# Preparing the factors of a Strassen product earlier and in smaller pieces, in a kernel of attention and two feed-forward networks

## The chip, the core and the metric

The kernel runs on one core of a Trainium2 chip. The metric is the device time of one execution in microseconds (us). Median, lowest and highest of three runs are given, and one further execution was profiled.

## The reference

Attention with keys and values pooled by eight, then a product of two linear layers, then a softplus network. All in float32; eight of the inputs are drawn eight times larger.

```python
k_p = k.reshape(B, H, Sp, 8, D).mean(axis=3); v_p = v.reshape(B, H, Sp, 8, D).mean(axis=3)
attn = softmax(q @ k_p.T / sqrt(D)) @ v_p          # B=8, H=8, S=576, D=64
x = attn.transpose(0, 2, 1, 3).reshape(4608, 512)
a = x @ w1; b = x @ w2                             # d_ff = 1024
x2 = (a * b @ w3) @ w_out                          # 512 wide
h = x2 @ w_in                                      # d_ff = 2048
out = (maximum(h, 0) + log1p(exp(-abs(h)))) @ w_out2
```

## The kernel before, in words

Every large product is made of three matmuls (`mm3`, L120): each operand is split into a rounded high part (copied by ScalarE, ACT) and the remaining low part (subtracted by VectorE, DVE), the pair that `split` (L115) issues. The weights arrive as 64-bit words and are converted by a chain of ACT and DVE operations.

**Phase 1** goes through nine blocks `j` of 512 tokens, each in eight units `i`. A unit (`p1_step`, L490) is 24 matmuls of 512 columns for a and b (`ab`, L455), then 12 matmuls of `x2_mm` (L475) for the unit before; w3 and w_out are multiplied into one matrix W at the start. a is copied from PSUM by ACT (L466), multiplied with b by DVE (L469) and split again. At the end of a block four results x2 are copied out (L485, L487) and stored to DRAM (L488). Between the three parts of a unit lie three slots. A slot calls what the hand-written list `sched` holds for it (attention of a later block) and then a number of steps of `background`, a list of generators whose step ends at each `yield`: `slot_1` (L500) makes one or two steps in turn, `bg_3` (L668) two or three. The list `sched` ends with unit 5 of block 7 (`i7` = 5). From there on the background is `late_jobs` (L613): eight `wi_job` (L566), which convert w_in, form the seven left factors of Strassen's method for one of eight column groups `t`, split them and store them to DRAM (`wis`), and eight `wo2_job` (L596), which convert w_out2. A `wo2_job` waits until the units of block 8 that read its memory are done. Before phase 2, L684 makes all remaining steps up to the fourth `wo2_job`.

**Phase 2** (loop at L766) goes through 48 steps `n`: six superblocks `s` of 768 tokens, eight groups `t` each. A step has seven products of six matmuls with 384 columns (`product`, L701), which accumulate in turn in the two PSUM tiles X and Z, and parts of the last product (`o_part`, L734), six matmuls of 512 columns each. After product 0, X is copied by ACT to a snapshot (L781) before product 2 may go on in X; after product 1, Z is added by DVE (L786) before product 3 may go on in Z, and so on (L797, L804, L809, L815, L822). The softplus of the step before (`soft_ops`, L712) runs on ACT and DVE meanwhile. Left factors come from DRAM by DMAs that GpSimd issues (`load_factors`, L535).

The seven right factors of a superblock come from x2, loaded by `x2_load` (L629) at t = 1, in steps of `x2_steps` (L650): four subtractions of 768 columns and seven splits. They lie in eight places of a ring. Three of the steps come at the end of t = 3, 4 and 5, the other six all within t = 7 (`xstep`, L771). In step n = 0 the last twelve matmuls of `x2_mm` stand ahead of product 2:

```python
                if n == 0:
                    next(xs)
                    x2_mm(NB - 1, K1 - 1)
                    load_factors(1, 1)
                product(n, 2)
                nc.scalar.activation(snap[1], xz[0], AF.Copy)
```

Every engine works its instructions off in the order written; loads and stores other than those of the left factors are issued by SyncE (SP), whose queue is in order too.

Of the kernel before, what the change touches and what calls it, by code (L numbers as in the profile page):

```python
# [15 lines left out]
P = 128  # L16
# [32 lines left out]
def pooled_attention_two_ffn(ctx: ExitStack, tc: tile.TileContext, qT_d, kT_d, v_d, w12_d, w3T_d, wo_d, wi_d, wo2_d, out):  # L49
# [141 lines left out]
    def add_group(src, slot, name, into):  # L191
# [8 lines left out]
        add_job(name, [src[:, 2 * i:2 * i + 2, :] for i in range(2)], dst)  # L200

# [172 lines left out]
    with tc.manual_schedule():  # L374
# [74 lines left out]
        background += [next_job() for _ in range(5)]  # L449
# [40 lines left out]
        def p1_step(j, i, slots):  # L490
# [5 lines left out]
            if (j, i) != (0, 0):  # L496
                x2_mm(*((j, i - 1) if i else (j - 1, K1 - 1)))
# [28 lines left out]
        F8 = F2 // 2 // P  # L526


        wis = [[dram.tile([P, 2, n, 256], F32, name=f"wis{t}_{n}", tag=f"wis{t}_{n}") for n in (3, 4)] for t in range(F8)]
        fin = ctx.enter_context(tc.tile_pool(name="fin", bufs=1))  # L530
        wf = fin.tile([P, 20 * 256], F32R, tag="wf", name="wf")
        y2 = fin.tile([P, 1024], F32, tag="y2", name="y2")
        wgroup = {}

        def load_factors(n, i):  # L535
            if n < F8 * NS:
                w = mem(GBUF + 8, [P, 2048], F32R) if (n % 2, i) == (1, 1) else wf[:, (0, 1536, 3584)[2 * (n % 2) + i]:][:, :(1536, 2048)[i]]
                wgroup[n, i] = w.rearrange("p (h c f) -> p h c f", h=2, f=256)
                nc.gpsimd.dma_start(wgroup[n, i], wis[n % F8][i].bitcast(F32R))

        t2k_ring[0] = Ring([T2K + 8 + 2 * i for i in range(4)])
        wo2_hl = {}


        EARLY = F8 + 4

        def load_rawl(n, srcs):
            raw = mem(RAW if n >= EARLY or n % 2 == 0 else RAW + 8, [P, 1024, 2], I32)
            n = 1024 // len(srcs)
            for i, src in enumerate(srcs):  # L550
                nc.sync.dma_start(raw[:, n * i:n * i + n, :].rearrange("p n t -> p (n t)"), src.bitcast(I32))
            return raw

        def convert_1024(raw, y):
            yi = y.bitcast(I32)
            nc.scalar.activation(y, raw[:, :, 1].bitcast(F32), AF.Abs, scale=HI_SCALE)
            yield
            nc.vector.tensor_scalar(y, y, HI_MIN, HI_MAX, op0=ALU.max, op1=ALU.min)
            nc.vector.tensor_scalar(yi, yi, 3, None, op0=ALU.logical_shift_left)
# [331 lines left out]
```

## Time and profile before

| | |
|---|---|
| median of three runs | 1651.43 us |
| lowest and highest | 1647.8 and 1652.45 us |
| the profiled execution | 1652.47 us |
| its span, from first to last instruction | 1650.7 us |
| PE busy in the span | 1551.8 us (94%), 7712 matmuls |
| DVE, ACT busy | 1001.8 us (61%), 786.6 us (48%) |
| mean granted TensorE clock | 0.978 |

Times in views count from the span's start. PE is TensorE's matmul stream, PEld its weight loads. A busy time of PE is modelled and overlaps, so the distance between starts of matmuls is the better measure. PEclk is the clock that was granted to TensorE, as a share of full speed.

### The profile page before, as it was taken

What the parts mean: (1) busy time and instruction counts of PE and PEld (TensorE: products, weight loads), DVE (VectorE), ACT (ScalarE), POOL (GpSimd) and SP (SyncE); (2) the same over time, 40 slices, a digit from 0 to 9 for tenths busy, and PEclk for the clock granted to TensorE, in tenths of its full rate; (3) what the DMA queues carried; (4) which work ended last, traced back from release to release, by engine and by line L of the source; (5) the groups of instructions that cost most, each with busy time, mean ns of one, the idle gap of its engine ahead of it and who ended that gap; (6) DMA issues with size and microseconds to landing.
All of it is one profiled execution on the core that took longest, in us unless ns stands there. A gap on an engine that the chain in (4) does not pass through costs nothing.

```text
span 1650.7 us, 20063 instructions
## 1 busy us (share of the span) xinstructions
PE 1551.8 (94%) x7712; PEld 1297.0 (79%) x7712; DVE 1001.8 (61%) x1490; ACT 786.6 (48%) x1651; POOL 53.6 (3%) x104
## 2 busy tenths in 40 slices
PE   4899999999999999898858999999999999999998
PEld 2457888888888887776647888898988988898997
DVE  7886534243423343348777877676677777677665
ACT  3454433343334343334345565556555555556554
POOL 0000000000000000000000000000000000000000
PEclk9999999999999999999978999999999999999999
DMA  8752212021202120219846435334434533533431
GB/s 272 223 164 72 89 35 87 18 85 35 75 21 74 35 75 1 77 58 354 276 141 209 134 115 178 122 108 155 145 117 145 171 116 120 180 109 115 147 115 39
DMA packets 64416, 198.44 MB, mean 120 GB/s; under 512 B 6464, under 2 KB 21824, under 8 KB 57152
## 3 DMA queue, kind: packets, MB, share of 16 engines
q1 hardware_dynamic: 50496, 109.07, 20.1%
q0 software_dynamic: 13824, 88.09, 16.4%
q8 instruction: 61, 1.00, 0.3%
q14 instruction: 35, 0.29, 0.1%
HBM read 163.58 MB, written 33.55 MB: 119 GB/s over the span
## 4 chain that ended last, share of the span: by engine, by line
PE 63%; DVE 19%; ACT 10%; DMA 5%; issue 2%; SPq 1%; DVEq 0%; ACTq 0%
PE ab L122 7%; PE ab L124 6%; PE ab L123 6%; PE o L747 5%; PE o L746 5%; PE o L745 5%; DVE area_r L118 4%; PE x2p L122 3%; PE x2p L124 3%; PE x2p L123 3%; PE X L122 3%; PE X L124 3%; PE X L123 3%; ACT area_r L117 2%; ACT area_f L717 2%; PE pv L303 2%
## 5 line engine op out<-in xcount | busy, mean ns | idle before, releaser
L117 ACT ACTIVATE area_r<-area_f 128x768 fp32r<-128x768 f32 (+1 forms) x168 | 126.7, 754 | 244.5 <-DVE area_f L469 175.8
L747 PE MATMUL o<-w2h,area_r 128*128 128x512 f32 x576 | 229.4, 398 | 0.3 <-DVE area_r L118 0.3
L746 PE MATMUL o<-w2l,area_r 128*128 128x512 f32 x576 | 228.8, 397 | 0.0
L745 PE MATMUL o<-w2h,area_r 128*128 128x512 f32 x576 | 225.8, 392 | 0.0
L118 DVE TENSOR_TENSOR area_r<-area_f,area_r 128x768 fp32r<-128x768 f32 (+1 forms) x168 | 141.7, 844 | 110.4 <-ACT area_r L117 110.2
L717 ACT ACTIVATE area_f<-area_f 128x768 f32<-128x768 f32 x96 | 81.3, 847 | 122.3 <-DVE area_f L815 120.8
L747 PEld LDWEIGHTS o<-w2h,area_r 128*128 128x128 f32 x576 | 109.0, 189 | 24.0 <-DVE area_r L118 0.7
L122 PE MATMUL X<-area_r,wf 128*128 128x384 f32 x288 | 100.8, 350 | 26.3 <-ACT xr L781 18.0
L745 PEld LDWEIGHTS o<-w2h,area_r 128*128 128x128 f32 x576 | 109.2, 190 | 16.2 <-ACT area_r L117 0.3
L746 PEld LDWEIGHTS o<-w2l,area_r 128*128 128x128 f32 x576 | 109.0, 189 | 16.0
L122 PE MATMUL x2p<-area_r 128*128 128x512 f32 x288 | 116.6, 405 | 5.2 <-ACT area_r L117 4.0
L469 DVE TENSOR_TENSOR area_f<-area_f,ab 128x512 f32<-128x512 f32 x72 | 49.4, 686 | 106.7 <-PE ab L124 105.0
L123 PE MATMUL x2p<-area_r 128*128 128x512 f32 x288 | 113.1, 393 | 0.2 <-DVE area_r L118 0.2
L124 PE MATMUL x2p<-area_r 128*128 128x512 f32 x288 | 113.2, 393 | 0.0
L268 ACT ACTIVATE pr<-sc,mx 128x72 f32<-128x72 f32 x288 | 87.7, 331 | 47.1 <-DVE mx L266 47.0
L118 DVE TENSOR_TENSOR area_r<-pv,area_r 128x512 fp32r<-128x512 f32 x36 | 24.8, 689 | 136.4 <-ACT area_r L117 136.4
L123 PE MATMUL X<-area_r,wf 128*128 128x384 f32 x288 | 99.3, 345 | 0.0
L124 PE MATMUL X<-area_r,wf 128*128 128x384 f32 x288 | 99.2, 345 | 0.0
L726 DVE SCALAR_TENSOR_TENSOR area_f<-area_f 128x768 f32<-128x768 f32 x96 | 91.3, 951 | 0.0
L466 ACT ACTIVATE area_f<-ab 128x512 f32<-128x512 f32 x72 | 43.1, 598 | 90.3 <-PE ab L124 65.8
L122 PEld LDWEIGHTS X<-area_r,wf 128*128 128x128 f32 x288 | 55.5, 193 | 37.3 <-ACT xr L781 20.6
L718 ACT ACTIVATE area_f<-area_f 128x768 f32<-128x768 f32 x96 | 81.2, 846 | 3.1
(190 smaller groups left out, 3468.1 us busy)
## 6 DMA issues: line engine op xcount, KB each, us to landing
wf<-wis POOLq DMA_DIRECT2D x48, 768.0 KB, 4.6
wf<-wis POOLq DMA_DIRECT2D x24, 1024.0 KB, 5.2
area_r<-wis POOLq DMA_DIRECT2D x24, 1024.0 KB, 5.1
area_f<-in_wo_dram SPq DMA_DIRECT2D x24, 512.0 KB
kv<-in_kT_dram SPq DMA_DIRECT2D x32, 288.0 KB
q<-in_qT_dram SPq DMA_DIRECT2D x18, 512.0 KB
kv<-in_v_dram SPq DMA_DIRECT2D x32, 288.0 KB
x2d<-area_f SPq DMA_DIRECT2D x36, 256.0 KB
```

The lines of the kernel that those rows point to most:

```text
L117: nc.scalar.activation(hi, src, AF.Copy)
L118: nc.vector.tensor_sub(lo, src, hi.bitcast(F32))
L122: nc.tensor.matmul(ps, whi, xhi, start=first, stop=False, skip_group_check=resumed)
L123: nc.tensor.matmul(ps, whi, xlo, start=False, stop=False, skip_group_check=resumed)
L124: nc.tensor.matmul(ps, wlo, xhi, start=False, stop=last, skip_group_check=resumed)
L268: nc.scalar.activation(pr[:, h, :], sc[h // 4][:, h % 4, :], AF.Exp, bias=mx[:, h:h + 1], scale=SCALE, accum_out=sm[:, h:h + 1])
L717: nc.scalar.activation(e, c, AF.Abs)
L718: nc.scalar.activation(e, e, AF.Exp, scale=-1.0)
L726: nc.vector.scalar_tensor_tensor(c, c, 0.0, e, op0=ALU.max, op1=ALU.subtract)
L745: nc.tensor.matmul(oacc[s][i], hl[:, 0, ts], wh, start=first, stop=False)
L746: nc.tensor.matmul(oacc[s][i], hl[:, 0, ts], wl, start=False, stop=False)
L747: nc.tensor.matmul(oacc[s][i], hl[:, 1, ts], wh, start=False, stop=last)
```

## The change

The left factors are prepared by a new generator `left_factors` in the background of phase 1, behind the last conversions of w1 and w2, in halves of 512 columns with two stage buffers, and their loads and the first x2 load are issued when attention ends. From then on the ring of phase 1's temporaries has four places and not eight. `bg_3` is gone: the last eleven units use `slot_1`. The generator `wo2_jobs` converts w_out2 for t = 0 to 5 there and in a loop ahead of phase 2, and for t = 6, 7 in halves during phase 2. Of block 8's `x2_mm`, units 4 to 7 are not run in phase 1 but as eight halves in the places that `o_part` leaves empty in steps 0 and 1. The right factors are spread: one step of `x2_steps` each in t = 3, 4, 5 and 6, three in t = 7, two in t = 0 of the next superblock; the ring has a ninth place. The snapshots and x2's halves have tiles of their own.

```diff
+    wis = [[dram.tile([P, 2, n, 256], F32, name=f"wis{t}_{n}", tag=f"wis{t}_{n}") for n in (3, 4)] for t in range(F8)]
...
+    def left_factors():
+        t2k_ring[0] = Ring([T2K + 8 + 2 * i for i in range(4)])
...
+        for _ in range(8):
+            yield
+        nc.sync.dma_start(raw.rearrange("p n t -> p (n t)"), wi_d[0].rearrange("p q k f -> p (q k f)").bitcast(I32))
+        yield
+        for t in range(F8):
+            yield from convert_1024(raw, y)
+            if t + 1 < F8:
+                nc.sync.dma_start(raw.rearrange("p n t -> p (n t)"), wi_d[t + 1].rearrange("p q k f -> p (q k f)").bitcast(I32))
+            a11, a12, a22, a21 = (y[:, 256 * i:256 * i + 256] for i in range(4))
+            s2, s3, s1, s4 = (S[:, 256 * i:256 * i + 256] for i in range(4))
+            nc.vector.tensor_add(s1, a21, a22)
+            nc.vector.tensor_sub(s3, a11, a21)
+            yield
+            nc.vector.tensor_sub(s2, s1, a11)
+            nc.vector.tensor_sub(s4, a12, s2)
+            yield
+            w3_, w4_ = wis[t]
+            for src, dsts in (
+                (y[:, :512], [w3_[:, :, 0:2, :]]),
+                (y[:, 512:768], [w4_[:, :, 2, :]]),
+                (S[:, :512], [w3_[:, :, 2, :], w4_[:, :, 0, :]]),
+                (S[:, 512:], [w4_[:, :, 1, :], w4_[:, :, 3, :]]),
+            ):
+                n = src.shape[1]
+                st = stage([P, 2, 512])[:, :, :n]
+                hi = st[:, 0, :].bitcast(F32R)
+                nc.scalar.activation(hi, src, AF.Copy)
+                yield
+                nc.vector.tensor_sub(st[:, 1, :].bitcast(F32R), src, st[:, 0, :])
+                n //= len(dsts)
+                for i, dst in enumerate(dsts):
+                    dst = dst.rearrange("p h c f -> p h (c f)") if len(dst.shape) == 4 else dst
+                    nc.sync.dma_start(dst, st[:, :, n * i:n * i + n])
+                yield
...
-        background += [next_job() for _ in range(5)]
+        background += [next_job() for _ in range(5)] + [left_factors()]
...
-        def x2_mm(j, i):
+        def x2_mm(j, i, ms=range(KD)):
...
-            hi, lo = g_hl.pop((j, i))
-            for m in range(KD):
+            hi, lo = g_hl[j, i]
+            for m in ms:
...
-                    sb = t2k(f"x2s{j}_{m}")
+                    sb = o_ring([P, 512]) if j == NB - 1 else t2k(f"x2s{j}_{m}")
...
-            if (j, i) != (0, 0):
+            if (j, i) != (0, 0) and (j, i) <= (NB - 1, K1 // 2):
                 x2_mm(*((j, i - 1) if i else (j - 1, K1 - 1)))
...
-        wf = fin.tile([P, 20 * 256], F32R, tag="wf", name="wf")
-        y2 = fin.tile([P, 1024], F32, tag="y2", name="y2")
+        wf = fin.tile([P, 2, 7 * 512], F32R, tag="wf", name="wf")
...
+        c_ring = {0: Ring([0, 3]), 1: Ring([6])}
+        e_ring, us = Ring([9, 12]), (mem(15, [P, TS]), mem(18, [P, TS]))
+        o_ring = Ring([21, 23])
...
-        EARLY = F8 + 4
...
-        def wi_job(t, raw):
...
-        def wo2_job(t, raw):
-            while (NB - 1, 2 * (t // 2) + 1) not in p1_done:
...
+        def wo2_jobs(ts, ys, raws, parts):
...
+            seq = [(t, p) for t in ts for p in parts]
...
+            for n, (t, p) in enumerate(seq):
+                while (NB - 1, 2 * (t // 2) + 1) not in p1_done:
+                    yield
+                raw, y = raws[n % len(raws)], ys[n % len(ys)]
+                yield from convert_1024(raw, y)
...
+                hi, lo = (w[:, p[0]:p[-1] + 1, :].rearrange("p i f -> p (i f)") for w in w2)
+                nc.scalar.activation(hi, y, AF.Copy)
                 yield
...
+                nc.vector.tensor_sub(lo, y, hi.bitcast(F32))
...
-        xq_ring = Ring([XODD + 6 * i for i in range(8)])
+        xq_ring = Ring([XODD + 6 * i for i in range(8)] + [GBUF + 8])
...
-        def bg_3():
-            att = slot_now[0]
-            slot_now[0] += 1
-            bg((2, 3)[att % 2])
+        load_factors(0, 0)
+        load_factors(0, 1)
+        load_factors(1, 0)
+        load_factors(1, 1)
+        x2_load(0)
+        background.append(wo2_jobs(range(6), [mem(T2K, [P, 1024]), mem(T2K + 4, [P, 1024])], [mem(RAW + 8 * i, [P, 1024, 2], I32) for i in range(2)], [(0, 1)]))
         for i in range(i7, K1):
-            p1_step(NB - 2, i, [bg_3] * 3)
-        xs = None
+            p1_step(NB - 2, i, [slot_1] * 3)
+        xs = x2_steps(0)
         for i in range(K1):
-            p1_step(NB - 1, i, [bg_3] * 3)
+            p1_step(NB - 1, i, [slot_1] * 3)
             p1_done.add((NB - 1, i))
-            if i >= 4 and xr:
-                xs = xs or x2_steps(0)
-                for _ in range(3):
-                    if len(xq.get(0, [])) < 5:
-                        next(xs)
-        while late_done[0] < EARLY:
+            for _ in range((2, 1, 1, 0, 1, 1, 1, 0)[i]):
+                next(xs)
+        while background:
             bg(1)
+        background.append(wo2_jobs((6, 7), [mem(25, [P, 512])], [mem(27, [P, 512, 2], I32)], [(0,), (1,)]))
+        rest = [(i, ms) for i in range(K1 // 2, K1) for ms in ((0, 1), (2, 3))]
...
-        o_ring = Ring([RAW + 14, T2K, T2K + 2])
...
+            if n < 0 and rest:
+                i, ms = rest.pop(0)
+                x2_mm(NB - 1, i, ms)
...
-                oacc[s] = [acc_tile(f"o{s}_{i}") for i in range(4)] + [mm_tile(f"o{s}_{i}") for i in (4, 5)]
+                oacc[s] = [mm_tile(f"o{s}_{i}") for i in range(2)] + [acc_tile(f"o{s}_{i}") for i in range(2, TT)]
...
             s, t = divmod(n, F8)
             h = n < NH
-            last_t = t == F8 - 1 and s + 1 < NS
-            def xstep():
-                if last_t:
-                    next(xs)
+            if n == 2:
+                o_ring = Ring([21, 23, 25, 27, 29])
+            if h and t == 3 and s + 1 < NS:
+                xs = x2_steps(s + 1)
+            def factors(*when):
+                if h and t in when and (s if t < 3 else s + 1) < NS:
+                    next(xs, None)
...
                 product(n, 0)
                 nc.scalar.activation(snap[0], xz[0], AF.Copy)
+                factors(0)
             soft_step(n - 1, 0)
             soft_step(n - 1, 1)
             if h:
                 product(n, 1)
                 nc.vector.tensor_add(soft[n, 0][:, :HS], snap[0], xz[1])
-                xstep()
             o_part(n - 2, 0, 0)
+            factors(0, 7)
...
             o_part(n - 2, 0, 2)
+            factors(3, 4, 5, 6, 7)
...
             o_part(n - 1, 1, 1)
             soft_step(n, 1)
             soft_step(n, 0)
             o_part(n - 1, 1, 2)
+            factors(7)
             bg(1)
-            if h and s + 1 < NS:
-                if t == 1:
-                    x2_load(s + 1)
-                if t == 3:
-                    xs = x2_steps(s + 1)
-                if t in (3, 4, 5):
-                    next(xs)
+            if h and t == 1 and s + 1 < NS:
+                x2_load(s + 1)
```

## Rows read from the trace of the kernel before

**Rows 1.** Windows: us; PE, PEld, DVE, ACT, POOL busy (count); PEclk; DMA share; GB/s

```profile
125.00:200.00 75.00, 72.60 (x405) 59.47 (x404) 47.10 (x90) 36.44 (x116) 0.00 (x0) 0.98 0.24 76
200.00:650.00 450.00, 450.00 (x2448) 369.35 (x2447) 168.47 (x304) 168.00 (x579) 0.00 (x0) 1.00 0.17 52
...
722.11:837.07 114.96, 98.47 (x397) 78.68 (x396) 85.75 (x115) 41.61 (x52) 1.72 (x3) 0.93 0.75 257
837.07:889.06 51.99, 30.96 (x115) 26.16 (x114) 37.43 (x45) 26.12 (x37) 2.65 (x5) 0.77 0.54 183
889.06:988.33 99.27, 95.85 (x469) 83.78 (x467) 79.99 (x101) 58.74 (x83) 6.67 (x12) 1.00 0.40 135
```

**Rows 2.** Waits of PE, 722.11 to 889

```profile
PE ab L122 <- ACT area_f L466: 11.7, 3, 6.6
PE X L122 <- ACT xr L781: 8.7, 1, 8.7
PE X L122 <- DVE area_f L809: 5.5, 2, 5.2
```

**Rows 3.** Timeline of PE, 24 matmuls apart: start us, us, line

```profile
640.86 0.39 PE L122 MATMUL ab<-area_r,w_6h 128*128 128x512 f32 x1
...
646.30 0.39 PE L122 MATMUL x2p<-area_r 128*128 128x512 f32 x1
```

**Rows 4.** Windows of steps n=8, 9 and 24, columns as in group 1

```profile
988.33:1007.76 19.43, 17.58 (x78) 15.44 (x79) 13.15 (x18) 11.23 (x16) 1.06 (x2) 0.91 0.27 89
1007.76:1023.40 15.64, 15.64 (x79) 14.07 (x78) 11.46 (x16) 8.90 (x15) 1.05 (x2) 1.00 0.74 233
...
1246.73:1264.75 18.02, 16.16 (x79) 14.01 (x79) 12.76 (x17) 10.71 (x15) 1.38 (x2) 1.00 0.32 101
```

**Rows 5.** Groups by line, shapes apart: xcount, busy us, mean ns of one

```profile
L118 DVE TENSOR_TENSOR area_r<-area_f,area_r 128x512 fp32r<-128x512 f32 x72 | 49.8, 692 | 55.5 <-ACT area_r L117 55.5
L469 DVE TENSOR_TENSOR area_f<-area_f,ab 128x512 f32<-128x512 f32 x72 | 49.4, 686 | 106.7 <-PE ab L124 105.0 <-ACT kT L234 1.1 <-ACT area_f L466 0.5
...
L118 DVE TENSOR_TENSOR area_r<-xr,area_r 128x768 fp32r<-128x768 f32 x42 | 40.0, 954 | 31.5 <-ACT area_r L117 31.5
...
L117 ACT ACTIVATE area_r<-xr 128x768 fp32r<-128x768 f32 x42 | 34.8, 832 | 8.8 <-DMA xr<-x2d 8.8
...
L561 DVE SCALAR_TENSOR_TENSOR area_f<-area_f 128x1024 int32<-128x1024 int32 x12 | 14.7, 1222 | 0.2
...
L556 ACT ACTIVATE area_f<-area_f 128x1024 f32<-128x1024 f32 x12 | 13.6, 1135 | 1.3 <-DVE w2l L607 0.6 <-DMA area_f<-in_wi_dram 0.4 <-DMA area_f<-in_wo_dram 0.3
...
L607 DVE TENSOR_TENSOR w2l<-area_f,w2h 128x1024 fp32r<-128x1024 f32 x8 | 9.8, 1220 | 3.4 <-ACT w2h L603 3.4
...
L603 ACT ACTIVATE w2h<-area_f 128x1024 fp32r<-128x1024 f32 x8 | 8.4, 1055 | 18.6 <-DVE area_f L563 18.6
...
L558 DVE TENSOR_SCALAR area_f<-area_f 128x1024 f32<-128x1024 f32 x12 | 8.3, 689 | 6.7 <-ACT area_f L556 6.7
```

**Rows 6.** Timeline around the first wait for a snapshot

```profile
856.81 0.47 ACT L781 ACTIVATE xr<-X 128x384 f32<-128x384 f32 x1
...
857.33 0.69 PE L122 MATMUL X<-area_r,wf 128*128 128x384 f32 x1 [8.74 <-ACT xr L781]
...
861.34 0.37 PE L122 MATMUL X<-area_r,wf 128*128 128x384 f32 x1
```

**Rows 7.** Chain of waits at 861 us and at the end: start, us

```profile
861.53 6.54 DMA x2d<-area_f
...
1643.98 2.09 DMA out_dram<-area_f
```

**Rows 8.** Timeline of DVE in step n = 12

```profile
1059.47 0.55 DVE L786 TENSOR_TENSOR area_f<-xr,Z 128x384 f32<-128x384 f32 x1
```

**Rows 9.** Timeline of PE in step n = 6

```profile
962.39 0.44 PE L122 MATMUL Z<-area_r,wf 128*128 128x384 f32 x1 [1.08 <-DVE area_f L786]
```

**Rows 10.** Chain of waits at 755 us

```profile
755.91 6.21 DMA wis<-wih
```

More of the change, by code (lines that the diff above doesn't have):

```diff
@@ L536, in load_factors @@
             if n < F8 * NS:
-                w = mem(GBUF + 8, [P, 2048], F32R) if (n % 2, i) == (1, 1) else wf[:, (0, 1536, 3584)[2 * (n % 2) + i]:][:, :(1536, 2048)[i]]
-                wgroup[n, i] = w.rearrange("p (h c f) -> p h c f", h=2, f=256)
+                wgroup[n, i] = wf[:, n % 2, 1536 * i:1536 + 2048 * i].rearrange("p (h c f) -> p h c f", h=2, f=256)
                 nc.gpsimd.dma_start(wgroup[n, i], wis[n % F8][i].bitcast(F32R))
-        t2k_ring[0] = Ring([T2K + 8 + 2 * i for i in range(4)])
@@ L542, in pooled_attention_two_ffn @@
         wo2_hl = {}
-        EARLY = F8 + 4
[L547 to L559, printed above, removed]
-            yield
-            nc.vector.scalar_tensor_tensor(yi, raw[:, :, 1], -0x80000000, yi, op0=ALU.bitwise_and, op1=ALU.bitwise_or)
-            yield
-            nc.vector.scalar_tensor_tensor(yi, raw[:, :, 0], 29, yi, op0=ALU.logical_shift_right, op1=ALU.bitwise_or)
-            yield
@@ L596, in wo2_job @@
-        def wo2_job(t, raw):
-            while (NB - 1, 2 * (t // 2) + 1) not in p1_done:
-                yield
-            y = mem(T2K + 4 if t % 2 and t < EARLY - F8 else T2K, [P, 1024])
-            yield from convert_1024(raw, y)
-            hi, lo = (main.tile([P, 2, 512], F32R, tag=f"wg{x}{t}", name=f"w2{x}{t}") for x in "hl")
-            nc.scalar.activation(hi.rearrange("p i f -> p (i f)"), y, AF.Copy)
-            for i in range(2):
-                wo2_hl[t + F8 * i] = hi[:, i, :], lo[:, i, :]
-            yield
-            nc.vector.tensor_sub(lo.rearrange("p i f -> p (i f)"), y, hi.rearrange("p i f -> p (i f)").bitcast(F32))
@@ L609, in pooled_attention_two_ffn, with load_wo2 @@
-        late = [(wi_job, t, [wi_d[t].rearrange("p q k f -> p (q k f)")]) for t in range(F8)]
-        late += [(wo2_job, t, [wo2_d[(t + F8 * i) * P:(t + F8 * i + 1) * P, :] for i in range(2)]) for t in range(F8)]
-        late_raw, late_done = [], [0]
-        def late_jobs():
-            for n, (job, t, _) in enumerate(late):
-                while len(late_raw) < min(n + (2 if n < EARLY else 1), len(late)):
-                    late_raw.append(load_rawl(len(late_raw), late[len(late_raw)][2]))
-                yield from job(t, late_raw[n])
-                late_done[0] = n + 1
+        def load_wo2(raw, t, parts):
+            for n, i in enumerate(parts):
+                f = t + F8 * i
+                nc.sync.dma_start(raw[:, 512 * n:512 * n + 512, :].rearrange("p n t -> p (n t)"), wo2_d[f * P:f * P + P, :].bitcast(I32))
@@ L619, in late_jobs @@
                 yield
-        background.append(late_jobs())
-        xq_ring = Ring([XODD + 6 * i for i in range(8)])
+        xq_ring = Ring([XODD + 6 * i for i in range(8)] + [GBUF + 8])
         xq = {}
-        xr = []
         def x2_load(s):
-            if not xr:
-                xr.extend(fin.tile([P, 1536], F32, tag="stage", name=f"xr{i}", bufs=3) for i in range(3))
             for i in range(2):
@@ L791, in pooled_attention_two_ffn @@
             if h:
-                if n == 0:
-                    next(xs)
-                    x2_mm(NB - 1, K1 - 1)
-                    load_factors(1, 1)
                 product(n, 2)
                 nc.scalar.activation(snap[1], xz[0], AF.Copy)
-                xstep()
             soft_step(n - 1, 0)
@@ L816, in pooled_attention_two_ffn @@
                 soft_step(n, 1)
-                xstep()
             o_part(n - 1, 1, 0)
```

65 lines of the change are left out of this document (25 added, 40 removed).

## The prediction

> **What bounds the kernel now.** I read the windows by stage first [rows 1]. From 200 to 650 us PE is busy for all of 450 us and DVE for 168.5: phase 1 is bound by the matmuls. From 722.11 (unit 5 of block 7, the first without attention) to product 0 of step 0 PE is busy 98.5 of 114.96 us at a granted clock of 0.93, then 31.0 of 51.99 us at 0.77 until step 2 begins at 889.06; DVE is busy 85.8 of the first. There the list of waits [rows 2] shows PE waiting for a copy of a on ACT (11.7 us), a snapshot on ACT (8.7) and an addition on DVE (5.5). None of these is slow; they stand in their queues behind conversions.
>
> How much is lost? At full pace 24 matmuls start 5.44 us apart [rows 3], 0.2267 us each. Eleven units of 36 are 89.8 us. A phase 2 step without a stall takes 15.64 us [rows 4]; its 36 matmuls of the last product are 8.16, so the 42 of Strassen's are 7.48. Step 0 with the twelve of `x2_mm` should take 10.2, step 1 with 18 of the last product 11.56. Together 111.6, against 166.95 taken: **55.4 us lost**. Steps 2 to 7 took 99.27 [rows 1] for six times 15.64: 5.4 lost. Step 8, the first of a superblock, took 19.43 at a clock of 0.91: 3.79 lost; 16, 32 and 40 are within 0.02 of it, and 24 lost 2.38 [rows 4]: 17.5 in all. So 78 us are within the change's reach.
>
> **The change, part by part.**
>
> No matmul comes or goes. The 48 of `x2_mm` that move (10.9 us) cost the same in steps 0 and 1.
>
> *Left factors in phase 1.* They make 9 + 8 x 14 = 121 background steps, at 1.5 per slot 81 slots or 27 units, so at least 27 x 8.16 = 220 us, past the dense attention of the start and ending around block 4. One group t costs DVE two passes of 0.69, two of 1.22 and eight operations no longer than 0.69 [rows 5], at most 9.4 us; eight are 75, and raise DVE from 37% to 71% at most. ACT gets at most 31 us. Both have room; the cost could only be delay. From below it is zero, as PE had no idle in 450 us that could be won or that shows a near miss; from above, 2.4 us of idle in the 75 us from 125 on, where conversions ran beside dense attention and DVE was at 63% [rows 1], make 7 in 220. I take **+1**, since the attention there leaves a slot more. The loads and 48 stores go on SP's queue, where a store waits for its DVE operation and holds the x2 stores and attention's loads behind it; those have buffers ahead. With four temporaries instead of eight, a's copy in a new block waits for an x2 store, but PE needs it only one part-unit later.
>
> *The w_out2 jobs.* This is what remains of the 55.4. One job is 5.04 us of DVE (2 x 0.69 + 2 x 1.22 + 1.22), and DVE also waits for ACT's 1.06 us high part [rows 5]: 6.1 in six steps. The first may start after unit 1 of block 8, so of 36 steps 27 fall into its last six units (4.5 each, where `bg_3` made 7.5), and nine into the loop ahead of phase 2. Units 2 to 4 last 8.16 us and hold this. Units 5 to 7 have no `x2_mm` left and last 5.44. From the start of unit 5 DVE has 22.5 steps (22.9 us), three multiplications and low parts with ACT's high part between (0.69 + 0.69 + 0.63, 6.0 us), two low parts of right factors (1.9), and about 2 us of waiting for unit 5's matmuls: 32.8. The last low part (1.2) is not awaited, the snapshot's copy (0.47) [rows 6] is: 32. PE is there after 16.3 + two products (2.14) + one half of `x2_mm` (1.36) = 19.8. So **PE waits 12 us at product 2 of step 0**, as it did for 8.74 before [rows 6]. If other work covers every wait of DVE, 22.5 steps are 18.9 us, the sum is some 25, and 5 remain; with a late load of w_out2 14. I take 12, since in the loop nothing else is there to cover. After the old wait twelve matmuls took 4.0 us [rows 6] instead of 2.14: +2 for the clock.
>
> *The second half of x2 in step 1.* Only two buffers take four results, so the third copy (ACT) waits until the first store has landed. The first copy ends some 3.7 us into the step, the third result is there at 5.4, and product 5, at 8.1, needs the snapshot that stands behind the third copy. A store of this size landed in 2.09 us at the quiet end, and in 6.54 at 861 us beside a load of factors [rows 7]: no wait, or 3.6 us. I take **2**: loads of factors run here too, but no other store. The Trainium skill (DMA: Bandwidth & Descriptors, section Anatomy of one DMA) gives a fixed 2.0 us plus the bytes by 436 GB/s; for 256 KB that is an estimate of 2.6 us, by which this term would be 0 and the sum 2 lower. The same page (Issuing engines are not separate DMA queues) says that DMAs of SyncE and GpSimd share their 16 engines, which speaks for the longer row.
>
> One more us for the border of blocks 7 and 8, where the stores of factors no longer crowd the DMA queues. Left of the 55.4: 12 + 2 + 2 + 1 = 17, **-38.4**.
>
> *Steps 2 to 7.* Only four half-wide conversions are left. They can hit the addition of line 786: in step 12, which began at 1007.76 + 3 x 15.64 = 1054.68, it ended 5.34 us in [rows 8], and product 3 could start after three products and two parts of the last product (3.2 + 2.7 = 5.9), so the slack is 0.6. I leave 1 us lost: **-4.4**.
>
> *Right factors.* t = 7 has three splits instead of six (ACT 0.83, DVE 0.95 each [rows 5]), which removes the late snapshots. But the next step now has two, and the first stands ahead of the addition of line 786: 0.95 and a wait of 0.5 for its high part move its end from 5.3 to about 6.7, so product 3 waits about 0.9. In step 6 a conversion in that place cost 1.08 [rows 9]. Five times 0.9 stay of 17.5: **-13.0** (bounds: 0 and -17.5).
>
> The sum: -38.4 - 4.4 - 13.0 + 1.0 = -54.8. Against the profiled execution (1652.47, span 1650.7) that is 1597.7; the median of the runs is 1.0 lower, so I give **1597**.
>
> **The rivals.**
>
> A, more room than I see: PE waits only 5 us in step 0, and at the borders the product finds its addition done. 7 + 4.5 us less: 1585. For it: DVE was idle for over a quarter of step 9 [rows 4]. Against: its queue is in order, and the loop has nothing else to run.
>
> B, the waits move: the third copy waits 3.6 us and the clock falls again (+4), the borders keep half (+4), phase 1 costs 7 (+6): 1611. For it: 0.6 us of slack. Against: no wait anywhere in [rows 1]'s long window.
>
> C, slower than before: the two stage buffers of the left factors. The high part of every third piece stands on ACT behind the store of the piece two before, issued three background steps, or two slots (5.4 us), earlier. A store of factors took 6.21 us in the crowded stretch [rows 10], so ACT may stand for a us; PE is covered for another 5.4. It decides when stores land later than 10.9 us: at 13 each of 32 pieces would cost 2.2, 70 us, and the kernel 1666. The DMA queues at 0.17 there [rows 1] speak against it.
>
> D, the change doesn't do what it says: the stretch is bound by the w_out2 jobs and not by the left factors, DVE falls behind already in unit 2, PE stops several times and its clock with it, and 35 of the 55 remain: 1615.
>
> **How the numbers follow.** The forecast has 0.60, A 0.16, B 0.15, D 0.05, C 0.04. The predicted time is the forecast's. The range goes from just below A to just above B, 1583 to 1613, and leaves out C, D and the outer parts of A and B. About 0.3% (5 us) is what a measurement of this kernel can tell from no change; all cases but C lie far beyond it: faster 0.95, same 0.01, slower 0.04.
>
> **What would show it.** Right: the stretch from the end of attention to step 2 takes about 129 us; one wait of PE near 12 us for the first snapshot; first steps of superblocks near 16.5 with a short wait of Z for the addition; attention ends within 2 us of 722. Wrong: waits of PE in blocks 0 to 4; first steps still above 18; a wait above 4 us in step 1; or no wait in step 0.

## The result, and the profile after

| | before | after |
|---|---|---|
| median of the runs, taken side by side | 1651.94 us | 1608.55 us |
| lowest and highest | 1647.8 and 1653.07 | 1606.29 and 1609.22 |
| the profiled execution (its span) | 1652.47 (1650.7) | 1606.29 (1604.5) |
| mean granted TensorE clock | 0.978 | 0.991 |

The ratio is 0.974, with a 95% interval of 0.972 to 0.976: the kernel is 43 us faster. From profile to profile the span is 46.2 us shorter; the sum of the prediction was 54.8.

The windows of after by stage, against [rows 1] and [rows 4]; columns as there. They are 200 to 230 us, the same 200 to 650 as before, unit 5 of block 7 to product 0 of step 0, from there to step 2, steps 2 to 7, step 8 and step 16.

```profile
200.00:230.00 30.00, 26.83 (x150) 21.67 (x148) 18.67 (x31) 13.08 (x35) 0.00 (x0) 1.00 0.50 169
200.00:650.00 450.00, 445.70 (x2425) 365.43 (x2423) 227.13 (x401) 189.98 (x620) 0.00 (x0) 1.00 0.31 102
727.93:810.49 82.56, 82.24 (x362) 67.42 (x361) 39.66 (x49) 23.37 (x33) 0.14 (x1) 1.00 0.37 138
810.49:858.67 48.18, 32.17 (x151) 28.22 (x149) 31.55 (x41) 23.22 (x34) 2.13 (x4) 0.86 0.42 135
858.67:954.03 95.36, 94.99 (x468) 84.14 (x469) 74.76 (x103) 56.19 (x82) 6.35 (x12) 1.00 0.42 138
954.03:973.36 19.33, 17.48 (x80) 15.46 (x78) 13.55 (x18) 12.00 (x18) 1.06 (x2) 0.91 0.29 97
1082.84:1099.48 16.64, 15.93 (x79) 13.94 (x78) 12.62 (x16) 10.07 (x15) 1.06 (x2) 1.00 0.33 113
```

The third line is the gain. PE was idle for 16.5 of 114.96 us there before; now it is idle for 0.3 of 82.56, at full clock. Part of the stretch is shorter only because matmuls moved behind it, so the fair measure is the loss against full pace, taken as in the prediction. The two stretches up to step 2 are 111.6 us at full pace and took 82.56 + 48.18 = 130.7: **19.1 lost, where it was 55.4**. Steps 2 to 7 lose 1.5 (before 5.4). Step 8 loses 3.7, steps 16, 24, 32 and 40 about 1.0 each, together 7.7 (before 17.5).

The waits of PE over the whole execution, against [rows 2]: us in total, times, longest. Left out are the waits of the start, for W (the longest 17.3 us, before 16.9), and those of 1 us or less in total but one.

```profile
...
PE pTp L342 <- DVE pr L333: 15.7, 9, 4.4
PE X L122 <- ACT snap L786: 15.1, 1, 15.1
PE sc L311 <- DVE area_r L118: 12.2, 9, 3.6
PE Z L122 <- DVE area_f L792: 4.9, 6, 1.8
PE pv L360 <- ACT pT L343: 2.3, 1, 2.3
...
PE X L122 <- ACT area_f L821: 0.9, 1, 0.9
```

Nearly all that is left around the change is one wait of 15.1 us for the first snapshot. The `Z` line holds the first steps of the superblocks. But `pTp`, `sc` and `pv` are attention, and between 199 and 212 us they hold three waits, where before had none. The timeline of after shows these places, and one more in step 1: start us, us, engine, line, operation, and in brackets the idle time before it and what ended it.

```profile
194.63 1.12 ACT L209 ACTIVATE area_f<-area_f 128x1024 f32<-128x1024 f32 x1 [7.56 <-DMA area_f<-in_wi_dram]
...
199.55 1.04 PE L342 MATMUL pTp<-ident,pr 128*72 128x128 f32 x8 [1.95 <-DVE pr L333]
...
205.68 1.14 PE L360 MATMUL pv<-pT,vb 72*64 72x128 f32 x16 [2.34 <-ACT pT L343]
...
813.18 0.96 DVE L118 TENSOR_TENSOR area_r<-xr,area_r 128x768 fp32r<-128x768 f32 x1 [1.86 <-ACT area_r L117]
...
827.76 1.06 ACT L624 ACTIVATE w2h<-area_f 128x1024 fp32r<-128x1024 f32 x1 [4.12 <-DVE area_f L216]
828.73 0.47 ACT L786 ACTIVATE snap<-X 128x384 f32<-128x384 f32 x1
...
829.25 0.69 PE L122 MATMUL X<-area_r,wf 128*128 128x384 f32 x1 [15.11 <-ACT snap L786]
...
855.97 0.66 ACT L209 ACTIVATE area_f<-area_f 128x512 f32<-128x512 f32 x1 [4.33 <-DMA area_f<-in_wo_dram]
...
858.67 0.45 PE L122 MATMUL X<-area_r,wf 128*128 128x384 f32 x1 [0.90 <-ACT area_f L821]
```

Around 200 us ACT stands 7.56 us for the first load of w_in (L209 is the first operation of a conversion). Attention's operations are queued behind it on ACT and wait, then PE does. The last matmul of attention comes at 724.06 and not at 718.23. At 829 us the snapshot's copy (0.47 us of work) stands behind the high part of the last conversion of w_out2, whose chain on DVE ended only then. At the end of step 1 there is a smaller case of the first kind: ACT stands 4.33 us for a load of w_out2, a copy (L821) behind it is late, and PE waits 0.90.

### The profile page after: what moved, and what is told of

Read it like the earlier page. It is cut to its first block, busy times and chain, and to the rows that moved or that the text cites. A ratio compares the mean times of both kernels' runs of the same rounds, so it can differ in the third digit from the quotient of the medians.

```text
span 1604.5 us, 20024 instructions
## 1 busy us (share of the span) xinstructions
PE 1528.8 (95%) x7712; PEld 1282.9 (80%) x7712; DVE 1002.9 (63%) x1516; ACT 785.0 (49%) x1671; POOL 53.6 (3%) x104
## 3 DMA queue, kind: packets, MB, share of 16 engines
q0 software_dynamic: 13824, 88.09, 16.5%
## 4 chain that ended last, share of the span: by engine, by line
PE 71%; DVE 14%; ACT 9%; DMA 3%; issue 2%; SPq 0%; DVEq 0%; ACTq 0%
PE ab L122 7%; PE ab L124 7%; PE ab L123 7%; PE o L750 6%; PE o L749 6%; PE o L748 6%; DVE area_r L118 4%; PE x2p L122 4%; PE x2p L124 4%; PE x2p L123 4%; PE X L122 3%; PE X L123 3%; PE X L124 3%; PE Z L122 2%; PE Z L123 2%; ACT area_r L117 2%
## 5 line engine op out<-in xcount | busy, mean ns | idle before, releaser
L122 PE MATMUL X<-area_r,wf 128*128 128x384 f32 x384 | 130.1, 339 | 16.1 <-ACT snap L786 15.1
L717 ACT ACTIVATE area_f<-area_f 128x768 f32<-128x768 f32 x96 | 81.3, 847 | 122.2 <-DVE area_f L815 120.7
L721 DVE TENSOR_SCALAR area_f<-area_f 128x768 f32<-128x768 f32 x96 | 53.8, 560 | 122.1 <-ACT area_f L718 122.1
L123 PE MATMUL X<-area_r,wf 128*128 128x384 f32 x384 | 130.0, 339 | 0.0
L124 PE MATMUL X<-area_r,wf 128*128 128x384 f32 x384 | 129.7, 338 | 0.0
L597 POOL DMA_DIRECT2D wf<-wis x96 | 51.8, 541 | 1500.2 <-PE X L124 776.8
L122 PE MATMUL Z<-area_r,wf 128*128 128x384 f32 x288 | 97.0, 337 | 4.9 <-DVE area_f L792 4.9
L123 PE MATMUL Z<-area_r,wf 128*128 128x384 f32 x288 | 97.0, 337 | 0.0
L124 PE MATMUL Z<-area_r,wf 128*128 128x384 f32 x288 | 96.5, 335 | 0.0
```

The source lines that it names most:

```text
L122: nc.tensor.matmul(ps, whi, xhi, start=first, stop=False, skip_group_check=resumed)
L123: nc.tensor.matmul(ps, whi, xlo, start=False, stop=False, skip_group_check=resumed)
L124: nc.tensor.matmul(ps, wlo, xhi, start=False, stop=last, skip_group_check=resumed)
L717: nc.scalar.activation(e, c, AF.Abs)
L721: nc.vector.tensor_scalar(u, e, 1.0, None, op0=ALU.add)
```

## The experiments

The differences quoted are against the kernel after, unless another is named; line numbers in an experiment's rows are its own. Repeated runs of the kernel after lie within 1606.3 to 1609.2 us, so an experiment that was run once is read by its trace, at the place that its edit touches.

**The first load earlier.** Is it the load that was issued one background step ahead of its reader?

```diff
+        nc.sync.dma_start(raw..., wi_d[0]...)
         for _ in range(8):
             yield
-        nc.sync.dma_start(raw..., wi_d[0]...)
         yield
```

> The first load of w_in words is issued eight background steps earlier, ahead of the eight empty steps; nothing else changes. In the changed kernel ACT stood 7.56 us for this load, and PE waited 1.95 us at 199.55 (transpose, for DVE's normalisation) and 2.34 us at 205.68 (values product, for an ACT copy). Theory: both waits are the shadow of that one load, issued only one step ahead of the operation that reads it. Then both waits vanish, attention ends about 4 us earlier (values product of the last group at about 720 instead of 724.06) and the kernel gains 4 us. Rival: the conversions as such are too dense beside attention, or the ring of four temporaries makes a's copy wait for an x2 store. Then the waits stay at 4 us or move by a slot, and the end of attention stays at 724.

Measured: 1600.2 us, span 1598.4. Its windows, 200 to 230 and 200 to 650:

```profile
200.00:230.00 30.00, 30.00 (x166) 24.61 (x165) 18.17 (x34) 11.79 (x34) 0.00 (x0) 1.00 0.46 152
200.00:650.00 450.00, 449.05 (x2443) 368.60 (x2442) 223.19 (x396) 188.87 (x619) 0.00 (x0) 1.00 0.31 100
```

The three waits are gone, with nearly the same DVE and ACT work in the stretch. From the transposes at 178 us (before at 179.04, after at 177.90, here at 177.62) to the last matmul of attention it takes 540.3 us, against 546.2 after and 539.2 before. So the left factors themselves cost phase 1 **1.1 us**, and the placing of one load **5.9** (the theory had 4). The rival's ring of four is no part of it: a's copy still stands 2.6 to 4.3 us for an x2 store in three blocks of this run, and none of PE's remaining waits up to 650 us is for that copy.

**More background steps in block 8.** Two or three steps per slot there, as `bg_3` had:

```diff
+        def slot_2():
+            att_slot()
+            bg(3 - slot_now[0] % 2)
...
-            p1_step(NB - 1, i, [slot_1] * 3)
+            p1_step(NB - 1, i, [slot_2] * 3)
```

> In block 8 a slot makes two or three background steps in turn instead of one or two; nothing else changes. Theory: PE's wait of 15.11 us in step 0 comes from the nine steps that are left for the loop, while DVE is idle in units 2 to 4 (it was busy 39.66 of 82.56 us from 727.93 to 810.49). With 7.5 steps a unit all 36 fit into units 2 to 7, the loop is empty, DVE ends about 4 us after PE, the wait is 3 to 6 us and the kernel gains 9 to 12 us. Rival: DVE's total work bounds these units, and a denser queue only makes PE wait in units 5 to 7 instead, for a's copy and the multiplication: the wait in step 0 shrinks, new waits of PE in block 8 add up to about the same, and the time stays within 2 us.

Measured: median 1601.88, ratio 0.971 (0.968 to 0.973) to before. The waits of PE from 722 us on:

```profile
PE X L122 <- ACT snap L790: 5.5, 1, 5.5
PE Z L122 <- DVE area_f L796: 4.9, 6, 1.9
PE ab L122 <- DVE area_f L526: 2.5, 2, 1.3
...
PE ab L122 <- ACT area_f L523: 1.1, 1, 1.1
```

The long wait falls from 15.1 to 5.5, but `ab` now waits 3.6 us in block 8, as it did in [rows 2], and step 2 begins only 4.7 us earlier. So the theory is right for the long wait (5.5, where it had 3 to 6), and the rival for half of what that gave: of the 9.6 us, 4.7 are left at step 2. The median is 6.7 us lower, between the two.

**The two splits of t = 0 later.** Behind two parts of the last product, so that neither stands ahead of the addition (L792) for which product 3 waits:

```diff
                 nc.scalar.activation(snap[0], xz[0], AF.Copy)
-                factors(0)
...
             o_part(n - 2, 0, 1)
+            factors(0)
```

> At t = 0 the two right factors are split behind the first and the second part of the last product, where the first stood ahead of the addition after product 1. Theory: the wait of Z for that addition (0.7 us at the four later borders, 1.85 at the first) comes from this split alone. Then the waits vanish, the steps 16, 24, 32 and 40 take 15.6 to 15.8 us instead of 16.65, step 8 takes at most 16.5 instead of 19.33, and the kernel gains 5 to 7 us. Rival: ACT and DVE are late anyhow from the three splits of t = 7. Then the wait stays, or becomes one for a snapshot after product 2, and first steps stay at 16.3 to 16.7.

Measured: 1599.18, span 1597.4. Windows of its steps 8 and 16:

```profile
953.63:970.32 16.69, 15.94 (x80) 13.94 (x78) 13.09 (x17) 11.09 (x17) 1.06 (x2) 1.00 0.34 110
1079.80:1095.46 15.66, 15.66 (x80) 14.09 (x78) 12.52 (x16) 10.20 (x15) 1.05 (x2) 1.00 0.35 119
```

Step 16 is at full pace, and so are 24, 32 and 40 (15.63 to 15.64). Step 8 loses 1.0 instead of 3.7. The splits' place is the whole loss at four borders; at the first, moving them takes away 2.7 of 3.7.

**No conversion for t = 6, 7** in phase 2:

```diff
-        background.append(wo2_jobs((6, 7), ...))
+        for f in (6, 7, 14, 15):
+            wo2_hl[f] = wo2_hl[5 + f // F8 * F8]
```

> The last two groups of w_out2 are not converted; t = 6 and 7 use the converted words of t = 5, so the output of this kernel is not the reference's; no matmul is left out. Theory: step 8, the first border, took 19.33 us and not 16.65 because the half-wide conversions of steps 0 to 5 put the chain of softplus on ACT and DVE about 1.1 us behind PE, and nothing brings it back before the border. Then steps 6 and 7 take 15.64 (16.18 and 15.72 before), step 8 about 16.65 and the kernel gains 3 to 4 us. Rival: the first superblock is late for another reason, such as the stall in step 0 or the loads of factors. Then step 8 stays at 19 and only steps 2 and 6 change, by under 1 us.

Measured: 1602.86, span 1601.1. Windows of its steps 2 and 6:

```profile
859.69:875.33 15.64, 15.64 (x79) 14.08 (x78) 10.37 (x14) 8.69 (x13) 1.06 (x2) 1.00 0.52 177
922.25:937.89 15.64, 15.64 (x79) 14.08 (x78) 11.83 (x15) 9.02 (x14) 1.06 (x2) 1.00 0.35 116
```

After, these steps took 16.54 and 16.18. Here steps 2 to 7 lose nothing, and step 8 takes 16.64 like the other borders. So the 1.5 us of steps 2 to 7 belong to the four half-wide conversions, and so do 1.2 us of step 1 (14.24 us here, its full pace, and 15.43 after). The 2.7 us of step 8 go with these conversions as they went with the splits' place above: they need both, and the two gains must not be added.

**x2 back in phase 1, but for unit 7.** This undoes the part of the change that keeps eight halves for steps 0 and 1; two remain.

```diff
-            if (j, i) != (0, 0) and (j, i) <= (NB - 1, K1 // 2):
+            if (j, i) != (0, 0):
...
-        rest = [(i, ms) for i in range(K1 // 2, K1) for ms in ((0, 1), (2, 3))]
+        rest = [(i, ms) for i in range(K1 - 1, K1) for ms in ((0, 1), (2, 3))]
```

> Of block 8's x2 products only unit 7 is kept for phase 2 (its two halves stand in step 0); units 4 to 6 run in block 8 as before. The rest of the change stays. Theory: what ends the wait of PE in step 0 is DVE's chain of w_out2 conversions, which does not depend on these matmuls; the 36 matmuls (8.16 us) kept back are then done after the stall and not during it. So the wait shrinks from 15.1 to about 7 us, the snapshot is copied at nearly the same time after the end of attention, step 2 begins 5 to 8 us earlier and the kernel gains 4 to 8 us against 1608.55. Rival: the kept matmuls cover the softplus and the factor loads of the first two steps; without them steps 0 and 1 wait by as much as they got shorter, and the time stays within 2 us or gets worse by up to 5.

Measured: median 1608.29, ratio 0.973 (0.971 to 0.975): unchanged, as the rival says, though not for the reason that it gives. The trace shows why (timeline; L542 copies a result of x2, L209 begins the conversion for t = 6, L799 is the second snapshot):

```profile
833.05 0.69 PE L122 MATMUL X<-area_r,wf 128*128 128x384 f32 x1 [8.40 <-ACT snap L786]
...
839.95 0.69 DVE L542 COPY area_f<-x2p 128x512 f32<-128x512 f32 x1 [3.28 <-DMA x2d<-area_f]
...
843.34 0.66 ACT L209 ACTIVATE area_f<-area_f 128x512 f32<-128x512 f32 x1 [8.39 <-DMA area_f<-in_wo_dram]
843.90 0.48 ACT L799 ACTIVATE snap<-X 128x384 f32<-128x384 f32 x1
...
844.43 0.69 PE L122 MATMUL X<-area_r,wf 128*128 128x384 f32 x1 [5.12 <-ACT snap L799]
```

The matmuls back in block 8 give the chain of conversions more cover, and the wait falls to 8.40. But the x2 stores now go out just ahead of the w_out2 load for t = 6, and ACT stands 8.39 us for it with the snapshot behind. It is the stall of 194 us once more, at another place.

**The same with empty steps behind the loads**, to take that stall away:

```diff
                 load_wo2(raws[n], *seq[n])
+            if ts[0] == 6:
+                for _ in range(2):
+                    yield
...
                     load_wo2(raw, *seq[n + len(raws)])
+                    if t >= 6:
+                        yield
```

> Only unit 7's x2 kept for phase 2, as in the run that left the time unchanged, and two empty steps ahead of the first conversion for t = 6, one after each later load. Theory: that run cut the wait for the first snapshot from 15.1 to 8.4 us and gave it back because ACT stood 8.4 us for a load just issued in step 0, with 5.1 us of PE behind it; without that it is 4 to 6 us faster than it was, 1602 to 1604. Rival: the waits behind it come from fewer matmuls beside the softplus of steps 0 and 1, and stay: 1607 to 1609.

Measured: median 1604.73, ratio 0.972 (0.971 to 0.973); the waits of PE from 722 us on:

```profile
PE X L122 <- ACT snap L791: 8.4, 1, 8.4
...
PE X L122 <- ACT area_f L826: 4.6, 2, 3.6
```

The 5.12 us are gone, but the next load does the same in step 1 (3.6 us for L826, ACT standing 4.48 for w_out2). The median is 3.6 lower than without the empty steps, and the two intervals overlap. That the stall was the load is shown; what keeping x2 for later is worth without any such stall is not settled.

**The right factors as before.** Six splits in t = 7, none in t = 0 and t = 6:

```diff
-                factors(0)
+                if n == 0:
+                    next(xs)
...
                 nc.scalar.activation(snap[1], xz[0], AF.Copy)
+                factors(7)
```

and so on after each of the six copies and additions of a step, with t = 3, 4 and 5 at a step's end.

> The right factors go back to the old places (three steps at the end of t = 3, 4 and 5, six within t = 7); left factors, x2 halves and the first superblock's own factors stay as changed. Theory: the spreading alone brought the first steps of superblocks from 19.4 to 16.65. Then the four later borders take 19.4 us again with a wait of 1.8 to 1.9 for the snapshot, step 8 takes 19 to 21, and the kernel loses 11 to 14 us. Rival: part of it came from tiles and places (own tiles for the snapshots, other places for softplus), which stay. Then first steps take 17 to 18 and the loss is 3 to 7.

Measured: 1619.9, span 1618.1, 13.6 above the profiled run after. The longest line of its waits of PE (from 722 us on) and the windows of its steps 8 and 16:

```profile
PE X L122 <- ACT snap L786: 24.5, 6, 15.1
```

```profile
960.30:978.33 18.03, 16.19 (x79) 14.02 (x80) 12.77 (x17) 10.71 (x16) 1.40 (x2) 1.00 0.28 93
1087.89:1107.31 19.42, 17.55 (x79) 15.38 (x79) 13.14 (x18) 11.23 (x16) 1.05 (x2) 0.91 0.30 94
```

Besides the 15.1 there are five waits for a snapshot, one at each border, of 1.84 to 1.87 us. Steps 16 and 32 take 19.42 with them at a clock of 0.91, as step 8 in [rows 4]; steps 8, 24 and 40 take 18.03 to 18.06 at 1.00, as step 24 there. The five borders lose 14.8 us, where after they lose 7.7. From the start of step 0 to that of step 47 the run takes 9.8 us more than after; the other 3.8 of the 13.6 lie ahead of step 0, where the edit changes nothing. So the spread of the right factors is worth about 10 us here, less than the theory's 11 to 14 and more than the rival's 3 to 7.

**The left factors late.** The generator starts at unit 5 of block 7, the rest stays, with two or three steps per slot as there were before:

```diff
-        background += [next_job() for _ in range(5)] + [left_factors()]
+        background += [next_job() for _ in range(5)]
...
+        background.append(late_factors())
         x2_load(0)
```

> The left factors are prepared from unit 5 of block 7 on, ahead of the w_out2 jobs, with two or three background steps per slot in these last eleven units, and their loads are issued when they are done; the rest of the change stays. Theory: the 8 x 14 steps are some 60 us of DVE that phase 1 hides. Here 82 steps find room in the eleven units and about 75 are left for the loop, so PE waits 50 us or more ahead of or in step 0, attention ends 5 us earlier, at about 718, and the kernel loses 35 to 50 us against 1608.55. Rival: block 8 has room for most of it, as DVE was busy only 39.66 of 82.56 us there; then the loss is 10 to 20 us.

Measured: 1679.95, span 1678.2: 71 to 74 us slower, more than either theory. The lines of its PE waits, of its window 815 to 905 and of its timeline (L250 makes a high part of left factors, L628 one of w_out2):

```profile
PE X L122 <- ACT snap L793: 84.6, 1, 84.6
```

```profile
815.00:905.00 90.00, 5.40 (x22) 4.75 (x22) 57.14 (x73) 26.30 (x34) 0.00 (x0) 0.53 0.50 176
```

```profile
831.54 1.11 ACT L209 ACTIVATE area_f<-area_f 128x1024 f32<-128x1024 f32 x1
...
842.92 1.29 ACT L250 ACTIVATE area_f<-area_f 128x512 fp32r<-128x512 f32 x2 [5.28 <-DMA wis<-area_f]
844.11 1.12 ACT L209 ACTIVATE area_f<-area_f 128x1024 f32<-128x1024 f32 x1
...
870.06 1.06 ACT L628 ACTIVATE w2h<-area_f 128x1024 fp32r<-128x1024 f32 x1 [4.01 <-DVE area_f L216]
...
876.26 1.06 ACT L628 ACTIVATE w2h<-area_f 128x1024 fp32r<-128x1024 f32 x1 [4.12 <-DVE area_f L216]
```

Nearly all of it lies in the loop ahead of phase 2. One group of left factors takes 12.6 us there (831.54 to 844.11), of which ACT stands 5.28 for a store to free one of the two stage buffers; one conversion of w_out2 takes 6.2. Three groups of left factors (38 us), 9 us in which ACT stands for the first load of w_out2, and 6 x 6.2 = 37 of w_out2 make the 84.6. The theory counted the steps in the loop well (about 75; three groups of 14 and six conversions of 6 are 78) and priced them too low, at 50 us or more. The run is 28 us slower than the kernel before, too: the old `wi_job` made eight steps per group, 64 in all, and `left_factors` makes 14, 112 in all, in slots that give 11 x 7.5 = 82 for these and for w_out2. So the run shows that the finer left factors don't fit at the old place; what the earlier place alone is worth, with the old steps, no run shows. The halves of 512 columns can be afforded only where there is a long stretch to spread them over. In the loop even the mechanism of rival C shows: 5.28 us of standing for the stage ring.

**The edits together, and w_out2 one conversion ahead.** The first two conversions are made before units of block 8 free their memory; only the high and low part wait for that.

```diff
+            for t in range(2):
+                yield from convert(t)
+            for t in range(6):
+                while (NB - 1, 2 * (t // 2) + 1) not in p1_done:
+                    yield
...
+                nc.scalar.activation(hi, ys[t % 2], AF.Copy)
+                yield
+                nc.vector.tensor_sub(lo, ys[t % 2], hi.bitcast(F32))
+                yield
+                if t + 2 < 6:
+                    yield from convert(t + 2)
```

> A version that puts the findings together: the first load of w_in early, both splits of t = 0 behind the addition, two or three background steps per slot in block 8, and the w_out2 jobs run one conversion ahead: the words of the first two are converted before their memory is free, and only the copy and the low part wait. Theory: 28 steps remain from unit 2 on and all are made by unit 6 or 7, so the loop is empty and DVE ends with PE; the wait in step 0 falls below 3 us, phase 1 gains 4 to 6 us and the borders 6.7: 1580 to 1586. Rival: DVE is behind in units 5 to 7 whatever the order; then waits of 5 to 8 us in all remain there and the time is 1587 to 1592.

Measured: median 1584.58, ratio 0.959 (0.957 to 0.961): faster than both kernels. No wait is left in step 0. Two lines of its timeline show what came in its place:

```profile
739.65 1.12 ACT L209 ACTIVATE area_f<-area_f 128x1024 f32<-128x1024 f32 x1 [12.40 <-DMA area_f<-in_wo_dram]
...
741.34 0.80 PE L122 MATMUL x2p<-area_r 128*128 128x512 f32 x1 [3.91 <-ACT area_r L117]
```

**The same without the faster rate** in block 8:

> The version with all edits, but block 8's slots keep their one or two steps. Theory: two of the six conversions of w_out2 lie ahead of unit 5, about 2 x 5.2 us of the chain, so the wait at the first snapshot of step 0 is 15.1 - 10.4 = about 5 us, and the time is about 5 us above the version with the faster rate: 1587 to 1592. Rival: the faster rate alone brought the wait to nothing, and without it 10 us or more of the 15.1 stay: 1595 or more.

Measured: 1592.21, span 1590.4, 6.4 above the span with the faster rate. The wait for the first snapshot is 3.4 us, so the 11.7 that went are the two conversions made ahead, and the rest needs the faster rate. The single run lies 0.2 us above the theory's range.

**The edits together, and patience behind each load.** As the version before last, with

```diff
             for t in range(2):
                 load_wo2(raws[t], t, (0, 1))
+            for _ in range(8):
+                yield
```

and one empty step behind each load for t = 6, 7.

> The version with all edits, and eight empty steps between the first w_out2 load and its conversion, one between each load for t = 6, 7 and the next conversion. Theory: an ACT that stands for a load which was just issued is what makes PE wait at 741 (3.9 us) and at 844.9 (1.35 us); both go, and the time falls by 4 to 5.5 us to about 1579 to 1581. Rival: the conversions are only late, and eight steps later the chain ends after block 8 again: the wait at the first snapshot of step 0 comes back with 4 us or more, and the time is 1584 or more.

Measured: median 1576.75 (1575.66 to 1580.32), ratio 0.955 (0.954 to 0.957), 74 us faster than the kernel before beside it, 32 faster than the change, and a little below the theory's 1579 to 1581. The longest of its waits of PE from 715 us on, and its windows from the last product of attention (unit 5 of block 7 begins 3.9 us later) to step 0, to step 2, and steps 2 to 7:

```profile
PE pTp L342 <- DVE pr L333: 1.6, 1, 1.6
PE X L122 <- ACT area_f L856: 1.0, 1, 1.0
PE Z L122 <- DVE area_f L826: 0.7, 1, 0.7
```

```profile
718.97:805.67 86.70, 86.06 (x390) 70.65 (x390) 53.50 (x64) 30.87 (x42) 2.26 (x4) 1.00 0.42 152
805.67:835.55 29.88, 29.88 (x151) 27.02 (x150) 20.29 (x30) 17.39 (x27) 2.13 (x4) 1.00 0.48 152
835.55:931.21 95.66, 94.65 (x469) 84.17 (x468) 74.04 (x102) 55.91 (x82) 6.34 (x12) 1.00 0.44 142
```

Steps 0 and 1 take 29.88 us, their full pace, and the clock stays at 1.00. Of the 78 us within reach 1.8 are left in steps 2 to 7 and about 1 at the first border.

## Why the prediction was right, and where its terms were off

The forecast (1597, range 1583 to 1613) named the right place, the right mechanism and the right next wait; 1608.55 lies within the range, between the forecast and rival B, for three terms that were too small: phase 1, the w_out2 jobs and the borders. Two of the signs that were named for a wrong forecast did appear, waits of PE in an early block and a first step above 18 us (step 8, 19.33), and attention ended 5.8 us later than before, where 2 was the limit. Against the sum, term by term, from profile to profile:

| term | predicted | measured |
|---|---|---|
| ahead of the left factors, up to the transposes at 178 us | 0 | -1.1 |
| left factors in phase 1 | +1 | +7.0 |
| left of 55.4 up to step 2 | 17 | 19.1 |
| left of 5.4 in steps 2 to 7 | 1 | 1.5 |
| left of 17.5 at the borders | 4.5 | 7.7 |
| steps behind the borders, and the end | 0 | -2.1 |

*Phase 1, +1.* The step that failed is "both have room; the cost could only be delay". There was room: with the first load earlier the left factors cost 1.1. What I did not price is that the first conversion stands on ACT for a load issued one background step before it. The load took 5.2 us in the chain of waits (189.39 to 194.55), ACT stood 7.56, and PE lost 5.9; with the 1.1 that makes the 7.0. I priced stores on SP's queue and found buffers ahead of them; I did not look at the distance from the new load to its reader. It was also wrong that the left factors run "past the dense attention of the start": the first conversion begins at 194.63, still within the dense stretch of 125 to 200 us; but with the early load that cost 1.1 at most.

*The w_out2 jobs, 12 us.* The wait came where it was forecast, for the copy that was named, with 15.1 us. The loop had 6.1 us per job by the prediction and 6.2 in the trace. PE was at product 2 20.9 us after unit 5 began at 793.21 (forecast 19.8), and the snapshot's copy ended 36.0 us after (forecast 32). The 4.0 us are these, by the trace. Four whole conversions and the end of a fifth lay on DVE from then on, 25.2 us at the prediction's price, where it counted 22.5 steps, 22.9 us: 2.3. Three low parts of right factors were in the way and not two: 0.95. And DVE stood 1.86 us at 813.18 for a high part that was queued on ACT behind that of a conversion, where a conversion alone makes it wait 1.12: 0.7. Its other waits came to the 2 us that I had allowed. The 2 us for the clock were right: after the wait the twelve matmuls of X and x2 took 4.3 us (829.25 to 833.51) instead of 2.4, and step 0 lost 2.0 besides the wait.

*The x2 store of step 1, 2 us.* PE had no wait for it. The first store was issued at 846.87, and the third copy, which needs its buffer, began at 849.37 as soon as its matmuls ended. The store was through in 2.5 us or less, at the end of the quiet row of [rows 7]. The Trainium skill's estimate of 2.6 us (DMA: Bandwidth & Descriptors, section Anatomy of one DMA — SWDGE (gpsimd) path) would have made the term 0, as it came out; the page gives its figures for DMAs that GpSimd issues, and this store is SyncE's. With x2 back in phase 1 the fourth copy stood 3.28 us for a store, so the other end of the range exists too, beside other transfers. Step 1 lost 1.2 us all the same, by a wait that the sum doesn't have: the one at 858.67 behind the load of w_out2.

*Borders, 0.9 each.* Steps 16, 24, 32 and 40 lost 1.0, and the run with the splits behind the addition shows that it is the 0.95 us split ahead of L792. Step 8 lost 3.7: it waits 1.85 us, and its clock is 0.91. The last operation of the conversions for t = 6, 7 ends in step 6 (at 924.9), but what stands behind it on the queues stays late: the addition of step 8 begins 7.34 us into the step, and 6.20 in the run without these conversions. I had put four half-wide conversions at 1 us in steps 2 to 7 and had not asked how long the queues stay behind after the last of them. Nor was the 1.08 us of [rows 9] the price of one conversion: between it and the last low part of w_out2 (L607, at 956.11 of before) stand, beside the softplus, two subtractions for right factors (L658, L659, 0.95 each).

*Rivals.* A (the wait of step 0 only 5 us) is what the conversions became with a faster rate, not in the change as it stands. B is right in one of its three parts: phase 1 cost its 7. C did not occur, but its mechanism is seen in the run with late left factors. D fell: PE does not stop in block 8, and the clock is 1.00 up to step 0.

## What to carry to other kernels

On an engine that works in order, a load needs its own lead in background steps: put the issue as many steps ahead as the landing takes by the trace, and let the reader come later rather than stand. When a chain moves off the critical path, sum what remains at its old place on the engines' queues, waits of one engine for another's queue included, and check how long the queues stay late behind its last piece; the transition gains only what the rest of the chain gives free. And a short operation that releases the matmul goes ahead of a long one that is only needed a step later.

## What the runs showed of the hardware

The loads of 512 KB took long to land beside other transfers, as the page of after has it among its DMA issues (KB each, median us to landing; 16 of the 24 are w_out2's, with the same median):

```profile
area_f<-in_wo_dram SPq DMA_DIRECT2D x24, 512.0 KB, 7.5
```

By the Trainium skill's figures for one DMA (the section named above, for DMAs that GpSimd issues) an estimate would be 2.0 + 1.2 = 3.2 us; these loads are SyncE's, and the measurement decides. ACT stood 4.2 to 12.4 us for such loads in the kernel after and in all experiments but two, the one without conversions for t = 6, 7 and the one with patience.

The granted clock can fall with a single short wait, and does not always. Steps with a wait of 0.71 us show 1.00 and lose 1.0. A wait of 1.84 to 1.87 us stands at all five borders of the kernel before and of the run with the right factors as before: six of these ten steps show 0.91 and lose 3.8 us, four show 1.00 and lose 2.4. Step 8 of after, with 1.85 us, is of the first kind, and of the run with x2 back in phase 1, also with 1.85 us, of the second (17.80 us). So a wait near 2 us costs its own length and then 0.3 to 0.6 us, or nearly 2 us more where the clock falls; which of the two comes, these runs do not explain. After 15.1 us of wait 810 to 859 us shows 0.86, and a stretch of 90 us with 22 matmuls 0.53, close to the lower of the two levels (1.2 of 2.4 GHz).
